# Skip weights of an S4 convolution moved from a VectorE add into the matmul group, one shared copy of the head matrices at the end, and another written-out order

## The chip, the cores and the metric

The kernel runs on one core of a Trainium2 chip. The metric is the device time of one execution in microseconds (us), the median of several runs; the kernel before takes 828.78 us (three runs, 824.48 to 829.89). The engines are TensorE (PE in the profile, its weight loads PEld), VectorE (DVE), ScalarE (ACT), GpSimd (POOL, which here issues the indirect gathers and the accumulating stores) and SyncE (SP, which issues the other DMAs).

## The reference

A layer normalisation feeds two branches, whose results are added to the input. Length 2048, width 448.

```python
def _A_ref(u, A_re, A_im, B_re, B_im, C_re, C_im, log_dt, Dskip):
    dt = jnp.exp(log_dt)[:, None]
    logdA = dt * (A_re + 1j * A_im)                       # 448 x 256 complex modes
    P = jnp.exp(logdA[:, :, None] * l[None, None, :])     # l = 0 .. 2047
    K = jnp.einsum("dn,dnl,dn->dl", Cc, P, dt * Bc).real  # one long filter per channel
    y = irfft(rfft(pad(u)) * rfft(pad(K)))[:L]            # causal convolution
    return y + u * Dskip                                  # the skip weights

def _B_ref(x, w_q, k1, k2, u, v):
    q = jnp.einsum("nd,dhc->nhc", xf, w_q)                # 16 heads, 2 halves of 256
    e = 64 * argmax(q1 @ k1.T) + argmax(q2 @ k2.T)        # one of 4096 experts per head
    act = gelu(einsum("nd,nhd->nh", xf, u[e]))
    return einsum("nh,nhd->nd", act, v[e])                # softmax over one entry is 1

xn = layernorm(x)
return x + _A_ref(xn, ...) + _B_ref(xn, ...)
```

`u * Dskip` is the same as a filter whose tap at lag 0 has Dskip added to it, and this is how both kernels do it.

## The kernel before

The work is cut into some 72 streams of steps. A step is a few instructions of one engine with the steps that it needs, the buffers that it takes and the buffers that it gives back. A string, `ORDER`, names a stream per character: in this order the steps are written, and so each engine's queue is filled. There is no scheduling at run time: an engine takes its queue in order, and an instruction whose semaphore is not there holds up everything behind it on the same engine. `Plan.run` walks the string and stops if a step stands before what it needs or finds no buffer left.

What the streams do:

- Set-up and weights (`c_*`, `par_*`, `w_*`): constants, the parameters of the modes, the query matrices multiplied with the keys.
- Branch B, scores (`ln_*`, `sc_*`, `u_*`), 16 tiles of 128 rows: normalise, transpose (L1000), score (L1019 and L1030), maximum and index on DVE and ACT. The indices go out to memory and come back.
- Branch B, experts (`e_*`, `o_*`): POOL gathers an expert's two rows per partition (L1148, 256 gathers), DVE takes the dot product (`e_d`, L1156), small steps make the gelu, PE adds the rows up (`e_p`, L1191), and POOL adds the tile to the output in memory (`o_st`, L1201).
- Branch A, filters (`s4_*`), 56 batches of 8 channels: ACT makes exponentials and sines (`s4_act`, L628, L630, L668 to L674), DVE phases and products (`s4_ph`, L653; `s4_v`, L699 to L705, into tiles `zi` and `mg`). Then the part that is changed, per batch: `s4_k1` (PE, L721) sums the products over the modes in 32 matmuls with 32 columns of weights each, into a tile of 128 x 128 in PSUM (`kp`, one of the three `kv` tiles); `s4_k2` (ACT, L729) copies 126 of the 128 columns to `kt`; `s4_k2b` (DVE, L732) adds the skip weights `dsk` to the other two columns, one for each group of four channels, writes them to `kt`, and gives back the PSUM tile; `s4_k3` (PE, L742) does the first stage of the Fourier transform on `kt`, and `s4_k4` (ACT, L746) copies it out.
- Branch A, convolution (`cv*`, `cu*`): in four chunks of channels, 128, 128, 128 and 64 wide. Products in the frequency domain (L846, L858; in the last chunk L805, L824, L832), the first inverse stage (`cv5`, L881 and L876), and its store to memory (`cv7`, tensor `t_d`).
- Branch A, end (`f_*`), per chunk four groups: SP loads a piece of `t_d` (L1214) and a piece of the head matrices `h` (L1216, 128 KB, two buffers `hl`); PE does the last stage (`f_p`, L1224); ACT copies (`f_a`, L1228); POOL adds it to the output in memory (`f_st`, L1233).

Every f32 matmul stands in the trace as two weight loads and two matmul passes.

Of the kernel before, what the change touches and what calls it, by code (L numbers as in the profile page):

```python
# [115 lines left out]
class Plan:  # L116
# [65 lines left out]
    "4444144HHHH0IIIIIIII2I2I4I2211412I264122622J4J7272HH1H7HLM2788LMLMII2L8MI444I22ZIII272I2844C4I4KOZ4IH4354C444443CPHH4DHN"  # L182
    "I46D4EEDEIJLCJCC779I79794M787DFD89L77FDFI7ECD4E79CEFEF4DK497C4N4EF44FDM84CR4CLEC9FZZD4878RQ44447DFEADCII7HHHHI97FR97I7K4"
    "M8K4IIIIIIIJD8EC5FLEC6FECDFDE7SSEDFFEFRRR77S9IIIAMOPSR9AxAAxANcQZZIIISSSTUUUIUURRIRBNJHHSSRRSIOSdIGPcxLRSSSTUUUUUUUUUHVW"
    "RWRaHRXGbISISMYRReIOIgSSIfIIIIfIKIPaxRLYGchhfSISRgSfTMRRyyyhhgIyfSSRQQzzRzOUzUyy!#!hh#yhK$gS$yJ%JPSzzyyhzz!LUSUhS#!JSThR"
    "y#Uiz$i$RyyUihh%yyyUUSRUUShURMRzZRzzS!#!OUhQ#UN$$UyyS%zSzzzSSifVWPhLWiRgRy!jTRx#f#H!$Ufh$U%SRifUSUhgMKJySRfiROKUhxhzGxyS"
    "SXxhkPzdiQzz!yYhS##SL!$$&zyMz%LTyzizUMe!j#hyUyzU!hHLy#UU$RUl$%UzRyiyUibzMKNdZUizLyRQyykhhhfSHeHMgL!#!VzzfRhiSlMLfzyS#fIN"
    "zhjRWyM!Yfg$#IRS#!IxhS$KS%I$SIihOgTIWI$PzhI%xNLRiUzIUIhcihIhRhMULQxxUI&hmmRNyyUzzyyy!yS##!$$%ziSZzzizkXRRMnihjSlhiSnHgRO"
    "y!YyahSzyyyy(J#f#Shkhgy!z$$%fflzzSPizhh!#fyjgR!hQiz#ZzLmkThlUidR$fUzMHiHHLRU$%IUyhReM!#IUSjI!#Uhh$hJh$%yISkUSUxIRbLKNhhU"
    "iy&cxlgRSMnOVhihPSy(yyyyyYizfzxcxzmzSg!S##iW!ThL1Rjnz$hIImUfz$kzz!U#fU%UyyyymNRlIUIMniySWRgSzfIRRI#zfQyROy!ShhI$i$%SzzZh"  # L190
    "zziZzhm!PJxSh##nzL!!$i#h#!$ShyMiS$Ri$Thj%HRnHxhL%MHRgNxUJfSiRLkhhgfUfiSyfUaiUlShUUSfhXiMRgKyROQxSiHzSIPRzSThUyhihjhkhUIy"
    "yIUyQyIIIRzdUzI&UzULMIeUSUzbIIjzzRlIhhkhR!SR#iSfyzhgRy!NKf#ahS$zh$ifygShN%OhgISJfSyy%VPLRhTf(zyyzRiMLUhMmhQiWiRzUylzizhn"
    "hizUmihSUyRh!#S#!hn$ym$UUjURnhyf%SifkySSlfUWJxYzfSiK%ROjghPNSyUyiymyhLnfgRhMLhgRT&xYQizRxxiziUzUzizyzz!MhUR#!yhjdyhz#$$%"
    "UzyySSR(RSzzU%hhkzyNyxiySbSkyOeSjSlPzRlihxRgzyiTXUixSzRRUShhh!khhgRylaUSUmnmR#UV!SyhfixzmOUSzUf#cS$zf$iU%S%hjyznWfiiWnUf"
    "gPKcTUzkyizhhhRRUySRhjSRRRiizhhQkhlmSlmUiyz!##yyyzyzoh!&hngh$$%yzhSSzSnzSiVfU%opgyfzTypyhzzqrhpgqphyUqhyrrifyq!rfi#f#hjs"
    "ooo!xi$i$%tkUythjyyhiyhihlbUpqkliiUyXrhhpfqg%pijhprhqfiqkghrixfrYohpdq&epgfriszfzxoxqhhhhzyUlzUzzzytjyyzhrpa!#z!#W$oW$zp"
    "zqhhtqzuyzyyUrhrgz%%pkzUfyhzflhqsif!hghihrUf#Uifitptpigi!qhyyy#pqmmi$r$i(yhyhhnyyyyhnj%kqmnhm%jnxyibhkuhrrlghszihhtxxxtV"
    "yKYylzzzyghzifziziWzzihmmfnngjiQhhkd!f#fzyyhefhiz&hyzzzlzh!hzuy!h#$i$#ifu#fica!hyjkghhl$y%ixj)g)$fxhfkh%ighhifhih**%%++h"
    "hmnixbzhhyzyyyyzYxzlizyiziz(jghhyykhz!mnyyyf&i(,dfijzifziz#lfzegkhhz#yygzlifh!hzhzh!$$mjmknhhn%hi#!mnhiil#hmn%ghhii)*+xg"
    "$hhijigyz$kff(cYfxx%%yziyyyyyyyzy(haflfhhjhhhy,yhghyhkhhyyxzzzbWiizz!iifglfmy,yfiz#!fzzi#iihhm&nzngjh$hhjf$khzh%kXao%dol"  # L200
    "zilmmhn)nzpxpoehqhyiizpgirypiqrf!f#qqph!hxxcrq#*+pry$$%fyhqpgjhrpqhYfzfgrpyrqsihhkhqhhi%tthzrihzplsXjdqhyriixczibztrtopi"
    "phifeqgzz,ihqhyyrufrzpqpqyy!krgphhflyupgm#rsfcYzfqyizhjyyy!&hqihhttrnkhzhhzrhhjsmanttklz#z$zziu$gh%iif%imffilhgf!ifinmhh"
    "ghjhdhb#i!e#y(knh$$yxhhxhxhyx%luhjg%hzhgkziyizyiyyyyyzzzyyhyhfifzmzizflyfzfigy!nz#yiimh)hhnhhjzk*+zhlhhhzmnjg)hhgz!kiz!#"
    "ififfi&f#!#$ljhhg)$iii$ifyk$%hjhhy,hhkhya*hhl*++%%hbixmnxghh%Y&xilgiijhhcfkiffgiifzhzhfihyhyjdkexzhyyyhzlhzzzmz!yy)nhhyy"
    ",yyz*ylg+hziiziifzhfzf#!yj#fiaghhfzz$y,ykzg!$i#yi#hihhm%%!hmhhnhnhbj$ik$hxdle%zYxog%iiizfljfhhgkhhgyixilmhnzf(ifihhmyfma"
    "xoyy,ynyjkzznlhmmznnzizhhpiqirpppqh!gijrhqhqprfipyhhyrqifpgqirph#!horgfsz#y&hzfzqhqh$f$%hrzyprhttpkijz%ilq(yyghqhzrhyhsb"
    "zh(rzfptktipxilhif!q#rqghrjohgfisok!hhf#fv$pihhixuohilthtqyyz$%yjgyphhhwq%iphhiripgkiffqiiuxrilqohhfzrfrfm&gnhvhijhhsmik"
    "hmhljtthhxvuizouzn(yyii)yyyyvhnkyiyizyyjwwilimnmknlmjwzmznklmzzzyyn(znpz!p#rp#rszzzz!tt!*+$rr#!p$s#)r$r$rr*ttsttstt+%u)u"
    "*%)%,*%&++,uu,(,))*+,)*)**+++,,,")


class Kernel:
# [473 lines left out]
    def products(s, b, B, e_, c1, c2, VK, col, u):  # L686
# [24 lines left out]
        def k1():  # L711
# [3 lines left out]
            for gi in range(G):  # L715
                n = 0
                for t in range(2):
                    for ri in range(2):
                        for c in range(4):
                            m = 32 * (NB * t + 4 * gi + c)  # L720
                            s.nc.tensor.matmul(kp[32 * c:32 * c + 32, 64 * gi:64 * gi + 64], T[ri][:, 1024 + m:1056 + m],  # L721
                                               view(T[ri], m, [[512, 2], [1, 32]]), start=(n == 0), stop=(n == 3))
                        n += 1


        j0 = JB[0]

# [570 lines left out]
```

## Time and profile before

| | |
|---|---|
| median of 3 runs | 828.78 us (824.48 to 829.89) |
| the profiled execution | 835.38 us, of which 833.6 us from the first to the last instruction |
| TensorE clock granted, mean | 0.892 of full speed |
| PE busy | 690.1 us, 83% of the span |
| DVE busy | 668.2 us, 80% |
| ACT busy | 546.2 us, 66% |
| POOL busy | 358.8 us, 43% |

The times of rows are from the profiled execution, which took 0.8% more than the median of the other runs. A row of a group gives the engine, the operation, the tile written and the tiles read, the shapes, the count, the busy time in us with the mean in ns of one instruction, and behind the bar how long the engine had been idle just before these instructions and what ended that. Matmuls overlap, so the busy time of a group of matmuls is less than count times mean. In a table by windows, each engine's busy time in the window stands with its count of instructions, then the granted clock, the share of DMA time and GB/s.

### The profile page before, as it was taken

The numbers are of one execution on the slowest core, as the hardware profiler recorded it, in microseconds if no ns is written. First come the engines' busy times: TensorE is split into PE (matmuls) and PEld (weight loads), VectorE is DVE, ScalarE is ACT, GpSimd is POOL, SyncE is SP. The second block draws the span as 40 slices with busy tenths as digits, with TensorE's granted clock in tenths as the row PEclk, the third lists the DMA queues.
The fourth block names the chain that finished last, engine by engine and source line by source line (L and its number), as shares of the span: only waits on it lengthen the run. The fifth ranks groups of instructions, "written<-read, shape, count | busy, mean of one in ns | idle before, by whom it ended". The sixth has DMA issues, their size and how long they took to land. (4 is left out here: it accounts for less than half of the span.)

```text
span 833.6 us, 19632 instructions
## 1 busy us (share of the span) xinstructions
PE 690.1 (83%) x7628; PEld 376.0 (45%) x7628; DVE 668.2 (80%) x1595; ACT 546.2 (66%) x1087; POOL 358.8 (43%) x307
## 2 busy tenths in 40 slices
PE   1999999999899997989989667758987777797982
PEld 0333443343444443434556344436753543675761
DVE  6695679999699998769889598878996988798630
ACT  5685337577485774544667486778895988796621
POOL 3101053547253555145425617674545286454214
PEclk9999999999899999889989876679995866998895
DMA  8998297889687769385886958999989599879679
GB/s 260 391 325 334 92 301 255 301 287 306 218 248 255 243 177 310 84 271 181 295 290 195 350 176 272 338 303 279 259 264 324 149 289 283 261 215 282 190 174 137
DMA packets 119093, 211.82 MB, mean 254 GB/s; under 512 B 38936, under 2 KB 94232, under 8 KB 118936
## 3 DMA queue, kind: packets, MB, share of 16 engines
q0 software_dynamic: 31232, 124.80, 48.1%
q1 hardware_dynamic: 87768, 85.77, 32.7%
q8 instruction: 60, 0.98, 0.5%
q14 instruction: 33, 0.27, 0.1%
HBM read 180.90 MB, written 33.29 MB: 257 GB/s over the span
## 5 line engine op out<-in xcount | busy, mean ns | idle before, releaser
L1148 POOL DMA_INDIRECT q<-in_uv_dram,ig x256 | 308.7, 1206 | 378.3 <-PE po L1191 154.5
L1019 PE MATMUL s<-q,xt 128*128 128x512 f32 x384 | 183.8, 619 | 1.8 <-ACT xt L1003 1.6
L1156 DVE SCALAR_TENSOR_TENSOR q<-q,xr 128x448 f32<-128x448 f32 x256 | 153.0, 621 | 5.1 <-DMA q<-in_uv_dram,ig 4.9
L1019 PEld LDWEIGHTS s<-q,xt 128*128 128x128 f32 x384 | 71.0, 194 | 94.5 <-issue 90.3
L721 PE MATMUL kv<-mg 128*32 128x64 f32 x1792 | 79.9, 245 | 32.2 <-issue 17.0
L721 PE MATMUL kv<-zi 128*32 128x64 f32 x1792 | 84.2, 244 | 18.1 <-issue 17.8
L628 ACT ACTIVATE mg<-kv 128x512 f32<-128x512 f32 x112 | 62.9, 601 | 30.1 <-PE kv L617 16.5
L721 PEld LDWEIGHTS kv<-mg 128*32 128x32 f32 x1792 | 52.4, 123 | 63.4 <-issue 34.7
L1191 PE MATMUL po<-q,A 128*32 128x448 f32 x512 | 69.5, 619 | 6.3 <-DVE A L1179 3.1
L721 PEld LDWEIGHTS kv<-zi 128*32 128x32 f32 x1792 | 56.9, 126 | 25.7 <-issue 25.6
L701 DVE TENSOR_TENSOR zi<-mg,CS 128x1024 f32<-128x1024 f32 x56 | 68.4, 1221 | 0.0
L705 DVE TENSOR_TENSOR mg<-mg,CS 128x1024 f32<-128x1024 f32 x56 | 68.3, 1219 | 0.0
L653 DVE CUSTOM_DVE_ANT_0 ph<-st,ph 128x512 uint16<-128x512 uint16 (+2 forms) x84 | 65.1, 775 | 0.2
L674 ACT ACTIVATE CS<-CS,halfpi 128x1024 f32<-128x1024 f32 x56 | 64.5, 1152 | 0.9
L1045 DVE TENSOR_REDUCE mx<-s 128x8 f32<-128x512 f32 x64 | 43.9, 686 | 25.3 <-PE s L1030 18.8
L668 ACT ACTIVATE CS<-ph 128x1024 f32<-128x1024 int32 x56 | 62.6, 1118 | 1.9 <-DVE ph L653 1.6
L671 ACT ACTIVATE CS<-ph 128x1024 f32<-128x1024 int32 x56 | 62.8, 1121 | 0.0
L742 PE MATMUL kv<-f,kt 128*64 128x128 f32 x448 | 41.2, 317 | 16.4 <-ACT mg L628 5.0
L765 PE MATMUL tp<-q,f 128*128 128x448 f32 x64 | 36.1, 648 | 19.5 <-DMA f<-in_f_dram 16.1
L699 DVE SCALAR_TENSOR_TENSOR zi<-mg,CS 128x512 f32<-128x512 f32 x56 | 38.6, 689 | 14.7 <-ACT CS L668 8.6
L617 PE MATMUL kv<-lc,rt 32*128 32x512 f32 x112 | 36.8, 568 | 14.1 <-ACT mg L628 7.1
L881 PE MATMUL s<-q,e 64*128 64x256 f32 x192 | 48.2, 404 | 0.0
(205 smaller groups left out, 1314.6 us busy)
## 6 DMA issues: line engine op xcount, KB each, us to landing
q<-in_wq_dram SPq DMA_DIRECT2D x32, 448.0 KB
xr<-xn_d SPq DMA_DIRECT2D x64, 224.0 KB
vu_d<-q SPq DMA_DIRECT2D x64, 112.0 KB
q<-vu_d SPq DMA_DIRECT2D x12, 512.0 KB
t_d<-q SPq DMA_DIRECT2D x24, 256.0 KB
q<-t_d SPq DMA_DIRECT2D x12, 512.0 KB
q<-in_uv_dram,ig POOLq DMA_INDIRECT x256
q<-in_x_dram SPq DMA_DIRECT2D x16, 224.0 KB
```

What stands on the lines that cost most here:

```text
L628: s.nc.scalar.activation(mg[:, :2, i], ps.rearrange("p (k n) -> p k n", k=2), AF.Exp)
L653: s.nc.vector.tensor_tensor(out=rw(n, 2 * n), in0=rw(0, n), in1=o["st"][:, k, b0:b0 + 2].rearrange("p b h m x -> p (b h m x)")[:, None].to ...
L668: s.nc.scalar.activation(CS[:, 1].rearrange("p (m r x) -> p m r x", r=16, x=2), four(s.ph), AF.Sin, scale=SC)
L671: s.nc.scalar.activation(B["CS"][:, 0].rearrange("p (m r x) -> p m r x", r=16, x=2), four(s.ph), AF.Abs)
L674: s.nc.scalar.activation(B["CS"][:, 0], B["CS"][:, 0], AF.Sin, scale=-SC, bias=s.halfpi)
L701: V.tensor_tensor(out=zi[:, 512:], in0=mg[:, 512:], in1=CS[:, 1], op=ALU.mult)
L705: V.tensor_tensor(out=mg[:, 512:], in0=mg[:, 512:], in1=CS[:, 0], op=ALU.mult)
L721: s.nc.tensor.matmul(kp[32 * c:32 * c + 32, 64 * gi:64 * gi + 64], T[ri][:, 1024 + m:1056 + m], view(T[ri], m, [[512, 2], [1, 32]]), start ...
L1019: s.nc.tensor.matmul(B["sc", q].rearrange("p a b -> p (a b)"), B["xt"][:, i], w, start=(q % 2 == 0 and i == 0), stop=(q % 2 == 1 and i == 2))
L1148: s.nc.gpsimd.indirect_dma_start(out=ue, out_offset=None, in_=s.io["uv"], in_offset=bass.IndirectOffsetOnAxis(ap=s.IDX[t][:, c, g:g + 1].b ...
L1156: s.nc.vector.scalar_tensor_tensor(Q["ue", g, c][:, :D], Q["ue", g, c][:, :D], 1.0, B["xr", c], op0=ALU.mult, op1=ALU.mult, accum_out=Q["d ...
L1191: s.nc.tensor.matmul(B["po"][32 * c:32 * c + 32, :D], Q["A"][:, g - g0, c], Q["ue", g, c][:, D:], start=(g == 0), stop=(g == 3))
```

## The change

Three edits.

First, `s4_k2b` is gone. Behind each group's 16 matmuls, `s4_k1` issues one more matmul that accumulates into the same PSUM tile: the 128 x 128 identity as weights, one column of `dsk` as the moving operand, one output column. So there are 112 such matmuls, and 56 DVE instructions fewer. `s4_k2` copies all 128 columns and gives back the PSUM tile; `s4_k3` waits for `s4_k2`.

Second, for the last two of the four chunks the head matrices come in one load of 512 KB (`f_h`), into one of the large `q` buffers, and the eight loads of 128 KB are gone; the buffer is held until the last `f_p`. The first two chunks load as before.

Third, the string `ORDER` is another one: 3217 steps where there were 3272 (56 `s4_k2b` fewer, one `f_h` more). Only its first line is shown.

```diff
 ORDER = (
-    "4444144HHHH0IIIIIIII2I2I4I2211412I264122622J4J7272HH1H7HLM2788LMLMII2L8MI444I22ZIII272I2844C4I4KOZ4IH4354C444443CPHH4DHN"
...
+    "4HH4HHIIIIIIIII1I1Z2I22220414IJJ14412142222274LM44LMLHMLHHH665M422222227424443K4C7788478H8II4OIIPDI44I3KI44NII44I47Z444I"
...
                             s.nc.tensor.matmul(kp[32 * c:32 * c + 32, 64 * gi:64 * gi + 64], T[ri][:, 1024 + m:1056 + m],
-                                               view(T[ri], m, [[512, 2], [1, 32]]), start=(n == 0), stop=(n == 3))
+                                               view(T[ri], m, [[512, 2], [1, 32]]), start=(n == 0), stop=False)
                         n += 1
-        j0 = JB[0]
+                s.nc.tensor.matmul(kp[:, 64 * gi + JB[0]:64 * gi + JB[0] + 1], s.ident, s.dsk[:, G * b + gi:G * b + gi + 1], start=False, stop=True)
 
         def k2():
-            s.nc.scalar.activation(B["kt"].rearrange("p (g j) -> p g j", g=G)[:, :, :j0], B["kp"].rearrange("p (g j) -> p g j", g=G)[:, :, :j0], AF.Copy)
-
-        def k2b():
-            s.nc.vector.tensor_tensor(out=B["kt"].rearrange("p (g j) -> p g j", g=G)[:, :, j0], in0=B["kp"].rearrange("p (g j) -> p g j", g=G)[:, :, j0],
-                                      in1=s.dsk[:, G * b:G * b + G], op=ALU.add)
+            s.nc.scalar.activation(B["kt"], B["kp"], AF.Copy)
             s.rel(B["kp"])
...
-        a1 = p.add("s4_k2", "ACT", ac(126), k2, deps=[a])
-        a = p.add("s4_k2b", "DVE", dv(2) + 4, k2b, port=False, deps=[a1, s.dskip_done], give=("kv",))
+        a = p.add("s4_k1", "PE", 1170, k1, deps=[v, s.dskip_done, s.C["ident"]], take=("kv", "kt"), give=("zi", "mg"))
+        a = p.add("s4_k2", "ACT", ac(128), k2, deps=[a], give=("kv",))
...
+        late = ck >= len(s.chunks) - 2
+        if ck == len(s.chunks) - 2:
+            def lh():
+                s.H = s.flat("q", "hall", 1024).rearrange("p (x e) -> p x e", e=32)
+                s.nc.sync.dma_start(s.H, s.io["h"])
+            s.h_done = p.add("f_h", "SP", xf(128, 4096), lh, deps=[s.t_done[ck - 1]], take=("ue",))
...
-                B["h"] = s.flat("hl", "hl", 256).rearrange("p (x e) -> p x e", e=32)
-                s.nc.sync.dma_start(B["h"], s.io["h"][:, 8 * g:8 * g + 8])
+                if not late:
+                    B["h"] = s.flat("hl", "hl", 256).rearrange("p (x e) -> p x e", e=32)
+                    s.nc.sync.dma_start(B["h"], s.io["h"][:, 8 * g:8 * g + 8])
```

What stands in the queues, at the places that the prediction speaks of. First PE at the `s4_k1` of the 37th batch, before (`kv` is the PSUM tile, `mg` and `zi` the products; x4 is one matmul for each of four column groups; `lc` and `rt` belong to the exponents, `ttl` to their load):

```order
L619 MATMUL kv2_106<-lc_134,rt_5026 128x256
L721 MATMUL kv0_104<-mg_5407 32x64 x4
L721 MATMUL kv0_104<-zi_5647 32x64 x4
L721 MATMUL kv0_104<-mg_5407 32x64 x4
L721 MATMUL kv0_104<-zi_5647 32x64 x4
L721 MATMUL kv0_104<-mg_5407 32x64 x4
L721 MATMUL kv0_104<-zi_5647 32x64 x4
L721 MATMUL kv0_104<-mg_5407 32x64 x4
L721 MATMUL kv0_104<-zi_5647 32x64 x4
L561 MATMUL kv2_106<-ident_123,ttl_5370 128x128 x2
```

And now, the same batch on the same engine:

```order
L616 MATMUL kv2_106<-lc_134,rt_5276 128x512
L720 MATMUL kv1_105<-mg_5416 32x64 x4
L720 MATMUL kv1_105<-zi_5677 32x64 x4
L720 MATMUL kv1_105<-mg_5416 32x64 x4
L720 MATMUL kv1_105<-zi_5677 32x64 x4
L723 MATMUL kv1_105<-dsk_131,ident_123 128x1
L720 MATMUL kv1_105<-mg_5416 32x64 x4
L720 MATMUL kv1_105<-zi_5677 32x64 x4
L720 MATMUL kv1_105<-mg_5416 32x64 x4
L720 MATMUL kv1_105<-zi_5677 32x64 x4
L723 MATMUL kv1_105<-dsk_131,ident_123 128x1
L618 MATMUL kv0_104<-lc_134,rt_5276 128x256
```

Two matmuls over the whole array have come into the batch, one behind each group of 16, and the step stands at another place among the exponents' matmuls.

Second, DVE about the same batch, before (L732 is `s4_k2b`, L1156 a dot product of the experts, L699 and L701 products of a later batch, L1166 to L1179 the small steps of the gelu):

```order
L1166 SCALAR_TENSOR_TENSOR x_5510<-x_5510,dot 128x8
L705 TENSOR_TENSOR mg<-mg,CS 128x1024
L1175 TENSOR_TENSOR dw<-dot,ig 128x8
L1172 SCALAR_TENSOR_TENSOR th<-th,dw 128x8
L1179 TENSOR_TENSOR A<-mask,th 128x256
L732 TENSOR_TENSOR kt<-kv_104,dsk 128x2
L1156 SCALAR_TENSOR_TENSOR q_80,dot<-q_80,xr 128x448
L1156 SCALAR_TENSOR_TENSOR q_79,dot<-q_79,xr 128x448
L699 SCALAR_TENSOR_TENSOR zi<-mg,CS 128x512
L701 TENSOR_TENSOR zi<-mg,CS 128x1024
```

And now (the lines are 1 to 7 lower):

```order
L1168 TENSOR_TENSOR dw<-dot,ig 128x8
L652 ISA ph<-st,ph 128x1024
L1165 SCALAR_TENSOR_TENSOR th<-th,dw 128x8
L652 ISA ph<-st,ph 128x2048
L1172 TENSOR_TENSOR A<-mask,th 128x256
L584 TENSOR_TENSOR st<-tpl,amt 128x16x32 x2
L698 SCALAR_TENSOR_TENSOR zi<-mg,CS 128x512
L1149 SCALAR_TENSOR_TENSOR q_86,dot<-q_86,xr 128x448
L700 TENSOR_TENSOR zi<-mg,CS 128x1024
```

The add is gone, and the first instruction behind the mask step that needs a result of ACT is now the product L698 (L699 before), with a step of the phases ahead of it instead of two dot products.

Third, the end of the program. POOL's last stores before (`ob` is a tile of the experts, `q` a group of the convolution; 4x128 is chunk three, 4x64 the last chunk):

```order
L1201 DMA out_dram<-ob 128x448
L1233 DMA out_dram<-q_98 128x4x128
L1233 DMA out_dram<-q_84 128x4x128
L1233 DMA out_dram<-q_103 128x4x128
L1201 DMA out_dram<-ob 128x448
L1233 DMA out_dram<-q_100 128x4x128
L1233 DMA out_dram<-q_92 128x4x64
```

And now:

```order
L1194 DMA out_dram<-ob 128x448
L1238 DMA out_dram<-q_103 128x4x128
L1238 DMA out_dram<-q_94 128x4x128
L1194 DMA out_dram<-ob 128x448
L1238 DMA out_dram<-q_90 128x4x128
L1238 DMA out_dram<-q_80 128x4x128
L1238 DMA out_dram<-q_84 128x4x64
```

The last tile of the experts (the second `ob`) is stored behind two groups of chunk three where it was behind three. On PE, too, its last matmuls stand ahead of the last `f_p` of chunk three, where one of their groups stood behind it. SP's last loads before (`t_d_116` is chunk three, `t_d_117` the last):

```order
L895 DMA t_d_117<-q_99 64x512 x2
L1214 DMA q_92<-t_d_117 128x8x64
L1216 DMA hl<-in_h_dram 128x256
L1214 DMA q_87<-t_d_117 128x8x64
L1216 DMA hl<-in_h_dram 128x256
L1214 DMA q_86<-t_d_117 128x8x64
L1216 DMA hl<-in_h_dram 128x256
L1214 DMA q_93<-t_d_117 128x8x64
```

And now:

```order
L1214 DMA q_103<-t_d_116 128x8x128
L1206 DMA q_96<-in_h_dram 128x1024
L1214 DMA q_94<-t_d_116 128x8x128
L1214 DMA q_90<-t_d_116 128x8x128
L888 DMA t_d_117<-q_83 64x512 x2
L888 DMA t_d_117<-q_97 64x512 x2
L1214 DMA q_80<-t_d_116 128x8x128
L888 DMA t_d_117<-q_79 64x512 x2
L888 DMA t_d_117<-q_99 64x512 x2
L1214 DMA q_84<-t_d_117 128x8x64
L1214 DMA q_102<-t_d_117 128x8x64
L1214 DMA q_100<-t_d_117 128x8x64
```

The one load of `h` stands behind the first load of chunk three, and the last chunk's four loads follow one another.

66 lines of the change are left out of this document (35 added, 31 removed).

## The prediction

> **What bounds the kernel now.** I read the page first, then busy time by stages, the waits, the groups of instructions, and last the timeline at single places. The chain of waits says nothing of the body: it reaches back only to 814 us. The stages say more (PE, PEld, DVE, ACT, POOL with counts, then clock, DMA share, GB/s):
>
> ```profile
> PE 690.1 (83%) x7628; PEld 376.0 (45%) x7628; DVE 668.2 (80%) x1595; ACT 546.2 (66%) x1087; POOL 358.8 (43%) x307
> 40.00:320.00 280.00, 268.67 (x1650) 113.41 (x1653) 244.51 (x618) 180.28 (x430) 105.68 (x88) 0.99 0.79 260
> 320.00:800.00 480.00, 383.62 (x5615) 244.36 (x5617) 398.57 (x926) 337.73 (x600) 233.49 (x193) 0.84 0.81 251
> 800.00:833.60 33.60, 15.82 (x296) 10.18 (x292) 0.86 (x2) 5.63 (x14) 10.18 (x9) 0.71 0.95 164
> ```
>
> From 40 to 320 us PE is busy for 268.67 of 280 us at a clock of 0.99: the score matmuls bound it. From 320 to 800 us nothing is full: DVE 83%, PE 80% at a clock of 0.84, ACT 70%. There the engines wait for one another in turn. The last 34 us are a tail of loads, small matmuls and stores.
>
> **What the add costs.** Its group, its spread over the two stages, and the waits that name it:
>
> ```profile
> L732 DVE TENSOR_TENSOR kt<-kv,dsk 128x2 f32<-128x2 f32 x56 | 8.9, 159 | 33.7 <-ACT kt L729 32.2 <-ACT mg L628 1.0 <-issue 0.4
> 40.00:320.00 280.00, 1.57 (x10) 0.99 0.79 260
> 320.00:800.00 480.00, 7.33 (x46) 0.84 0.81 251
> DVE kt L732 <- ACT kt L729: 30.0, 12, 7.3
> PE kv L742: 1.9, 1
> ```
>
> 56 adds of 159 ns are 8.9 us, 7.3 of them behind 320 us, where DVE also stood idle for 30.0 us in front of them, in 12 places (fourth row, waits of that stage). The last row is from the list of who waited for the add: PE lost only 1.9 us to it. All of 30 us is not to be had. The three longest of these waits (idle time in brackets), with ACT at the longest:
>
> ```profile
> 548.67 0.16 DVE L732 TENSOR_TENSOR kt<-kv,dsk 128x2 f32<-128x2 f32 x1 [3.39 <-ACT kt L729]
> 551.55 0.68 DVE L585 TENSOR_TENSOR st<-tpl,amt 128x512 int32<-128x512 int32 x1
> 633.39 0.16 DVE L732 TENSOR_TENSOR kt<-kv,dsk 128x2 f32<-128x2 f32 x1 [7.00 <-ACT kt L729]
> 634.69 0.69 DVE L699 SCALAR_TENSOR_TENSOR zi<-mg,CS 128x512 f32<-128x512 f32 x1
> 717.39 0.16 DVE L732 TENSOR_TENSOR kt<-kv,dsk 128x2 f32<-128x2 f32 x1 [3.68 <-ACT kt L729]
> 718.68 0.69 DVE L699 SCALAR_TENSOR_TENSOR zi<-mg,CS 128x512 f32<-128x512 f32 x1
> 632.81 0.38 ACT L565 ACTIVATE rt<-kv 128x256 fp32r<-128x256 f32 x1 [7.08 <-PE po L1191]
> 633.50 1.15 ACT L668 ACTIVATE CS<-ph 128x1024 f32<-128x1024 int32 x1
> ```
>
> At 633 us DVE waited for ACT, but ACT itself had stood for 7.08 us behind a late PE, and the sine L668 comes only then. Behind the add DVE had 634.69 - 633.55 = 1.1 us of dot products; then comes the product L699, which needs that sine. Without the add DVE does these 1.1 us early and waits at L699 instead. At 717 us the same: 718.68 - 717.55 = 1.1 us can move. At 548 us phases and dot products fill the time to 551.55 at least, 2.7 us of the 3.39. So 4.9 of 14.07 us, 35%, can be filled; the rest is ACT's and PE's lateness and reappears at L699. In the new order the product stands one phase step of this kind behind the mask step, which is no better.
>
> **The sum, part by part**, against the profiled execution of 835.4 us (span 833.6 and 1.8 around it); it is 0.8% above the median of 828.8, and the sum's difference is taken off the median.
>
> *DVE.* Relief behind 320 us: 7.3 us of adds and 35% of 30.0, 10.5, together 17.8 us. Bounds: 7.3 and 37.3. How much reaches the end is a choice: all of it if DVE were the bound, little where PE or ACT is. With DVE at 83% and PE at 80% side by side I pass 0.55: -9.8 us. In the first stage PE binds and covers the 1.6 us: nothing; were PE not the bound there, they would be gained too.
>
> *PE and ACT behind the add.* With it goes the hand-over ACT, DVE, PE: the 1.9 us for which PE waited, -1.9 (bounds 0 and twice that).
>
> *The identity matmuls.* 112 matmuls are 224 passes of 128 x 128 weights and one column. No row shows one column; the nearest, with the batch's own matmuls by stage last:
>
> ```profile
> L1000 PE MATMUL tp<-ident,q 128*128 128x128 f32 x64 | 10.2, 283 | 0.0
> L1000 PEld LDWEIGHTS tp<-ident,q 128*128 128x128 f32 x64 | 8.0, 147 | 10.0 <-issue 8.6 <-ACT pw L485 1.4
> L1019 PE MATMUL s<-q,xt 128*128 128x512 f32 x384 | 183.8, 619 | 1.8 <-ACT xt L1003 1.6
> 40.00:320.00 280.00, 14.86 (x704) 11.89 (x704) 0.99 0.79 260
> 320.00:800.00 480.00, 86.61 (x2880) 63.84 (x2880) 0.84 0.81 251
> ```
>
> A pass with 128 columns holds PE for 10.2 / 64 = 159 ns, one with 512 columns for 183.8 / 384 = 479 ns; so 0.83 ns a column, and 159 - 127 x 0.83 = 54 ns at one column, an estimate. 224 x 54 ns = 12.1 us of PE. The low end is a pass of the packed 32-column matmuls, (14.86 + 86.61) / 3584 = 28 ns, 6.3 us; the high end a pass that neither its load nor its drain hides, 147 + 283 = 430 ns, 96 us. A gain is excluded: the passes come on top, in the same queue. I take 54, since identity, weights and shape are those of L1000, which lies between the packed and the bare pass. By the packed matmuls' counts 11 of 56 batches lie in the first stage (704 of 3584): 2.4 us there count in full. The other 9.7 lie in a stage where PE is idle for a fifth of the time; a quarter of it passes, 2.4. Together +4.8 us. The idle time of PE is the cover; without it 12.1.
>
> [...]
>
> *The tail.* First the chain, then ACT, POOL, PE and SP:
>
> ```profile
> 814.35 1.42 DMA out_dram<-ob
> 815.77 5.63 issue
> 821.40 0.04 POOLq L1233
> 811.98 0.54 ACT L1198 ACTIVATE ob<-po 128x448 f32<-128x448 f32 x1 [4.73 <-PE po L1191]
> 813.59 1.27 POOL L1233 DMA_DIRECT2D out_dram<-q  x1 [4.77 <-ACT q L1228]
> 822.05 3.92 POOL L1233 DMA_DIRECT2D out_dram<-q  x3 [6.29 <-issue]
> 809.87 1.08 PE L1224 MATMUL kv<-q,hl 64*32 64x128 f32 x32
> 813.73 0.53 SPq L1214 DMA_DIRECT2D q<-t_d  x1
> 816.26 0.34 SPq L1216 DMA_DIRECT2D hl<-in_h_dram  x1
> 818.70 0.34 SPq L1216 DMA_DIRECT2D hl<-in_h_dram  x1
> ```
>
> The last tile of the experts was put out at 814.35, and the next store, to the same rows of the output, went at 822.05, 7.7 us later, with four behind it. In the new order one `f_p` (1.08 us) no longer stands ahead of that tile on PE, and one store of 813.59 no longer stands ahead of it on POOL (about 1.2 us between tile ready, 812.52, and its turn): -2.3 us if the 7.7 stay as they are. Shared `h` takes away SP's stops at 816.26 and 818.70 (2.5 and 2 us, for a buffer `hl`), so that the last four groups are ready ahead of POOL: that alone moves nothing, since POOL is later, but it keeps the gain. Its 512 KB go through SP ahead of the loads of chunk three, whose groups wait for it; at the 164 GB/s of that stage they take 3 us beside PE's work. I take -2.5. Bounds: 0, if the store's own 7.7 us stretch, and -5.
>
> *The order.* Its other effect is taken at nothing. What hides it: the steps are those of before. What it may do is bounded by the waits of DVE outside the add in the long stage, 480 - 398.6 - 30 = 51 us: a fifth of them, 10 us, either way.
>
> Sum: -9.8 - 1.9 + 4.8 - 2.5 = -9.4 us. 828.8 - 9.4 = 819.4, rounded to 819.
>
> **Rivals.** Changes below 1%, 8.3 us, can hardly be told from none.
>
> *The waits only move (28%).* For it: at 633 us ACT had been waiting as long as DVE. Then only the 7.3 us of adds remain, at 0.55 a gain of 4.0 instead of 9.8, and the hand-over gains nothing: 828.8 - 4.0 + 4.8 - 2.5 = 827. Against it: at 548 us there is work to fill the wait.
>
> *The waits go altogether (14%).* All 37.3 us of relief at 0.55, 20.5, instead of 9.8: 808 to 809. For it: the order may have put ready work ahead of every late one. [...] Against: ACT's own waits stay.
>
> *The identity loads break up the packed matmuls (17%, slower).* A load of all 128 columns may wait for the four column groups ahead of it and hold up the four behind it. With c ns a pass, a fifth in full and the rest at a half (the wait then lies in the batch's own chain), it costs 224 x c x 0.6; it eats the 14.2 us of gains from c = 106 ns on and makes the kernel slower by over 1% from 167 ns. Half of the bare 430 ns, 215, costs 28.9 us: 828.8 + 14.7 = 843 to 844. For it: PEld's 147 ns a load at L1000. Against: the same loads with their matmuls took 159 ns a pass, columns and all. [...]
>
> *The add isn't gone* can be left out: the queues show it gone.
>
> **The numbers.** The forecast has 41%; its own range, with the order's 10 us and the smaller bounds, is 808 to 831. The range over all is 807 to 838: it takes in the first rival, half of the second, and leaves out the most of the slower one. Faster by over 1%, below 820.5: somewhat over half of the forecast's 41% and nearly all of the second rival's 14, and some of the first's by the order, 0.42. Slower by over 1%, above 837: most of 17 and a little of the first, 0.18. Within: 0.40.
>
> **What would show it.** Right: DVE busy near 659 us; DVE's idle time behind 320 us down by 8 to 15 us and found at L698 and at the products of the convolution; the identity's passes near 54 ns of PE each; the last tile of the experts 2 us nearer to the last convolution matmul. Wrong: passes of over 100 ns, or a batch's sums that take much more than the 1.35 us (14.86 / 11) of the first stage; DVE's idle time unchanged; or waits for gathers on DVE, which the trace of before hardly has, by the new order.

## The result, and the profile after

The changed kernel is slower: 852.81 us (median of 4 runs, 851.28 to 860.5) against 829.34 us of the kernel before in the same session. The ratio is 1.0322, with a 95% interval of 1.0231 to 1.0413; like all ratios below it compares the runs in the faster of two states alone, so it is not the quotient of the two medians. The profiled execution took 854.22 us, 852.2 of them from the first to the last instruction. The forecast was 819.

First the page's busy times and the long stages of the kernel after, then the places where DVE waited in the long stage, behind 320 us:

```profile
PE 734.4 (86%) x7852; PEld 415.2 (49%) x7852; DVE 662.5 (78%) x1539; ACT 549.9 (65%) x1089; POOL 359.3 (42%) x307
```

```profile
40.00:320.00 280.00, 267.67 (x1574) 115.33 (x1574) 228.32 (x575) 170.18 (x401) 100.32 (x87) 0.98 0.76 248
320.00:800.00 480.00, 410.52 (x5485) 265.69 (x5484) 392.44 (x872) 344.00 (x609) 235.31 (x191) 0.83 0.81 249
```

```profile
DVE zi L698 <- ACT CS L667: 18.5, 5, 7.7
DVE q L851 <- ACT us L846: 18.3, 10, 5.9
```

And three rows of the same stage before:

```profile
DVE q L858 <- ACT us L853: 10.5, 9, 1.8
DVE zi L699 <- ACT CS L668: 8.6, 4, 4.8
DVE x L1166 <- ACT x L1163: 2.6, 4, 0.9
```

DVE does 5.7 us less than before (668.2), less than the 8.9 us of the add, since other groups took a little longer. But PE does 44.3 us more (690.1). In the long stage PE went from 383.62 to 410.52 us busy, while fewer of its instructions lie in that stage (5485 for 5615): the work has moved to the right, out of the stage. DVE's 30.0 us of waits at the add are gone, and two other waits have grown: at the product behind the sine from 8.6 to 18.5 us, and at the product of the convolution (`L851`, before `L858`) from 10.5 to 18.3.

Next the new group itself, matmul and weight load, and the page's chain of waits by line, which in this execution reaches back to the start and so says more than that of before:

```profile
L723 PE MATMUL kv<-dsk,ident 128*128 128x1 f32 x224 | 48.9, 286 | 0.5 <-issue 0.5
L723 PEld LDWEIGHTS kv<-dsk,ident 128*128 128x128 f32 x224 | 39.2, 219 | 13.8 <-issue 6.2
```

```profile
PE s L1012 21%; PE kv L720 10%; PE po L1184 6%; PE s L1023 4%; PE s L839 4%; PE kv L723 4%; PE kv L736 4%; PE tp L758 4%; PE s L874 4%; PE kv L616 3%; PE kv L909 2%; ACT CS L667 2%; ACT CS L670 2%; PE kv L618 2%; ACT CS L673 1%
```

One column of output holds PE for 48.9 / 224 = 218 ns a pass, four times the 54 ns of the forecast, and the identity matmuls are 4% of the chain, some 34 us. PE lines hold most of the chain.

The timeline shows where the time of one such matmul lies. This is PE at 301 us of the kernel after, at full clock (granted 1.00 from 300 to 302.5 us); x8 are eight passes in a row, and they overlap, so one reads the distance of the starts:

```profile
300.71 0.32 PE L720 MATMUL kv<-mg 128*32 128x64 f32 x8
300.85 0.29 PE L720 MATMUL kv<-zi 128*32 128x64 f32 x8
300.96 0.29 PE L720 MATMUL kv<-mg 128*32 128x64 f32 x8
301.07 0.29 PE L720 MATMUL kv<-zi 128*32 128x64 f32 x8
301.30 0.38 PE L723 MATMUL kv<-dsk,ident 128*128 128x1 f32 x2
301.61 0.32 PE L720 MATMUL kv<-mg 128*32 128x64 f32 x8
```

Eight packed passes follow one another every 0.11 us, so the identity's two passes would begin at 301.18; they begin at 301.30, 0.12 us late, and the packed ones go on at 301.61. Between 301.18 and 301.61 lie 0.43 us, in which PE would have done some thirty packed passes. It is not this place alone: over the whole trace the first load of an identity matmul begins a median of 148 ns behind the start of the packed pass ahead of it. What fills this gap no view shows; of two other shapes below one has it and one does not.

### The profile page after: what moved, and what is told of

It is laid out like the page before. It is cut to its first block, busy times and chain, and to the rows that moved or that the text cites. A ratio compares the mean times of both kernels' runs of the same rounds, so it can differ in the third digit from the quotient of the medians.

```text
span 852.2 us, 19988 instructions
## 1 busy us (share of the span) xinstructions
PE 734.4 (86%) x7852; PEld 415.2 (49%) x7852; DVE 662.5 (78%) x1539; ACT 549.9 (65%) x1089; POOL 359.3 (42%) x307
## 4 chain that ended last, share of the span: by engine, by line
PE 72%; ACT 13%; issue 6%; DVE 4%; DMA 2%; another core or an unknown queue 1%; POOL 1%; SPq 0%; POOLq 0%; ACTq 0%; DVEq 0%
PE s L1012 21%; PE kv L720 10%; PE po L1184 6%; PE s L1023 4%; PE s L839 4%; PE kv L723 4%; PE kv L736 4%; PE tp L758 4%; PE s L874 4%; PE kv L616 3%; PE kv L909 2%; ACT CS L667 2%; ACT CS L670 2%; PE kv L618 2%; ACT CS L673 1%
## 5 line engine op out<-in xcount | busy, mean ns | idle before, releaser
L1012 PE MATMUL s<-q,xt 128*128 128x512 f32 x384 | 186.8, 626 | 2.6 <-ACT xt L996 1.7
L720 PE MATMUL kv<-zi 128*32 128x64 f32 x1792 | 79.4, 244 | 12.4 <-issue 12.3
L720 PEld LDWEIGHTS kv<-mg 128*32 128x32 f32 x1792 | 48.7, 121 | 41.6 <-issue 29.0
L698 DVE SCALAR_TENSOR_TENSOR zi<-mg,CS 128x512 f32<-128x512 f32 x56 | 38.6, 690 | 30.7 <-ACT CS L667 18.5
L720 PEld LDWEIGHTS kv<-zi 128*32 128x32 f32 x1792 | 53.9, 126 | 17.5 <-issue 17.3
L736 PE MATMUL kv<-f,kt 128*64 128x128 f32 x448 | 43.7, 330 | 19.9 <-ACT mg L627 13.0
L851 DVE TENSOR_TENSOR q<-us,s 128x512 f32<-128x512 f32 x48 | 32.3, 683 | 25.3 <-ACT us L846 18.3
```

What stands on the lines that cost most here:

```text
L736: s.nc.tensor.matmul(vp[64 * ri:64 * ri + 64, 128 * gi:128 * gi + 128], B["kt"][:, 64 * gi:64 * gi + 64], s.f1[:, ri], start=True, stop=True)
L1012: s.nc.tensor.matmul(B["sc", q].rearrange("p a b -> p (a b)"), B["xt"][:, i], w, start=(q % 2 == 0 and i == 0), stop=(q % 2 == 1 and i == 2))
```

## The experiments

The runs fell on several chips of two kinds: on one kind the kernel before takes 824 to 830 us, as in the forecast's runs ("the first kind"), on the other 762 to 764 ("the second kind"). Each ratio is against the kernel before on the same chip.

**Theories.** A: the identity passes cost what they hold of PE, and about half of that reaches the end (the third rival of the forecast). B: the new order is at fault, and the passes happen to be there. C: the shared copy of the head matrices.

**The identity matmuls alone, and both orders without any skip weights.** The first kernel is the kernel before with the first edit only, in the old order (the `s4_k2b` steps struck from the string). The other two leave the skip weights out, in the new order and in the old. In all three, and in every later version without the add, `s4_k2` copies all 128 columns and gives back the PSUM tile, as in the kernel after.

```diff
 # old order, identity matmuls: edit one alone
+s.nc.tensor.matmul(kp[:, 64 * gi + JB[0]:64 * gi + JB[0] + 1], s.ident, s.dsk[:, G * b + gi:G * b + gi + 1], start=False, stop=True)
-p.add("s4_k2b", "DVE", ...)
 # new order without skip weights: the kernel after, and
-s.nc.tensor.matmul(kp[:, 64 * gi + JB[0]:64 * gi + JB[0] + 1], s.ident, ...)
 # old order without skip weights: the kernel before, and
-p.add("s4_k2b", "DVE", ...)
```

> The order of before with the identity matmuls in place of the DVE add (56 steps taken out of the string, the head loads as before). Theory A (the identity passes cost it: 224 passes of 218 ns in the trace of the changed kernel, 48.9 us of PE): 842 to 856 us, and L-row of the identity again near 49 us. Theory B (the new order costs it, the identity is hidden): 818 to 830 us.

> The changed kernel without the 112 identity matmuls: the skip weights are left out of the computation. Theory A: PE loses 49 us of busy time and the time falls to 810 to 828 us. Theory B: it stays at 838 to 852 us, since the order is what costs.

> The kernel before without the DVE adds: the skip weights are left out of the computation, the order of the other steps is unchanged. It measures the add by itself. If DVE's waits in front of the add go altogether: 800 to 812 us. If they only move, as the prediction's first rival has it: 821 to 829 us. By the prediction's own step (17.8 us of relief, 0.55 of it passed on, and 1.9): about 817.

Measured: old order with identity matmuls 1.025 (1.0159 to 1.0341); new order with none 0.9981 (0.9944 to 1.0019); old order with none 0.9894 (0.9842 to 0.9946). Later the two in the old order were run again, both on one other chip of the first kind, and the new order with none on a third:

> The old order with the identity matmuls, nothing else changed. On the 763 us chip: if the cost goes by the line's TensorE time, as in the new order (46 us of it, 3 per cent), 1.015 to 1.025 over before; if the new order is what makes the passes dear there, 1.00 to 1.01. On the 824 us chip it repeats 1.016 to 1.034.

> The kernel before with the skip weights left out (no add, no identity matmul; the output is short of them by intent). If this falls on a chip where the kernel before takes about 763 us: it is the base that the pieces in the old order lacked. If the passes cost by their TensorE time in the old order as in the new, the ratio is 0.985 to 0.992 (pieces at 28 us of TensorE stood at 1.0024, at 14.7 us at 1.0052). If the pieces cost nothing in the old order, it is about 1.00. On a chip where before takes 824 us it repeats 0.984 to 0.995.

> The new order without identity and without add once more (the skip weights are left out), with more rounds, to size the order against the old order without add, which was 0.9894 of before. If the new order and the shared head are worth nothing: 0.989 to 0.993. If the new order is itself worse by 1%: 0.996 to 1.002.

Measured: identity in the old order 1.0379 (1.0339 to 1.042), none in the old order 0.9976 (0.9942 to 1.0011), none in the new order 0.9995 (0.9923 to 1.0068). The same edit moves by about 1% from chip to chip, more than its intervals, so differences are best taken within one chip. The result's own chip is known only by its kind. The passes in the old order cost 1.025 - 0.9894 = 3.6% on the one and 1.0379 - 0.9976 = 4.0% on the other, 29 and 33 us, each within one chip; in the new order 1.0322 less 0.9981 or 0.9995 is 3.3 to 3.4%, 27 to 28 us, a difference across chips that has a like within one chip of the second kind below (3.05%). That is theory A, and B falls: the passes cost as much in the old order. The group in the old order, from the first of these runs, has the size of the one after:

```profile
L724 PE MATMUL kv<-dsk,ident 128*128 128x1 f32 x224 | 50.2, 292 | 2.5 <-issue 2.5
```

Where the add alone is gone (old order with none), the waits of DVE in the long stage read:

```profile
DVE x L1159 <- ACT x L1156: 12.2, 6, 5.2
DVE q L851 <- ACT us L846: 9.8, 6, 6.0
DVE zi L699 <- ACT CS L668: 9.5, 4, 4.9
```

The 30.0 us at the add are gone, and 12.2 us (14.2 in the second run) stand at another small step of the experts that before waited 2.6 us: so some of the wait was time that ACT lacked and only moved, as the first rival had it. The gain of 0.2 to 1.1%, 2 to 9 us, is what removing the add brought; the interval of the first run reaches 1.6%, that of the second 0.6%.

**The head matrices alone.** The kernel before with the second edit only, `f_h` written right behind the first load of chunk three.

```diff
+s.h_done = p.add("f_h", "SP", xf(128, 4096), lh, deps=[s.t_done[ck - 1]], take=("ue",))
 ...
+if not late:                                   # late: chunks three and four
     s.nc.sync.dma_start(B["h"], s.io["h"][:, 8 * g:8 * g + 8])
```

> The kernel before with the shared head matrices alone (the DVE add and the order of before kept, the one load of 512 KB put in behind the first load of chunk three). By the prediction's step on the tail, where SP's stops alone move nothing because POOL is later: within 1.5 us of before. If the eight loads and their two buffers set the end: 3 to 7 us faster.

Measured: 1.0011 (0.9969 to 1.0052), from 3 us faster to 4 us slower. C falls.

**Fewer or smaller passes in the old order.** In the first, one identity matmul per batch with two output columns in place of two with one; in the second, four tiles of 32 x 32 on the diagonal, which is all of the identity that is not zero. In every version with these matmuls once per batch, the second group of 16 also no longer opens with a clearing flag of its own (`start=(gi == 0 and n == 0)`).

```diff
 # one per batch, behind both groups
+s.nc.tensor.matmul(view(kp, JB[0], [[64, G]]), s.ident, s.dsk[:, G * b:G * b + G], start=False, stop=True)
 # four diagonal tiles per batch
+for c in range(4):
+    r = slice(32 * c, 32 * c + 32)
+    s.nc.tensor.matmul(view(kp[r], JB[0], [[64, G]]), s.ident[r, r], s.dsk[r, G * b:G * b + G], start=False, stop=True)
```

> The order of before, no DVE add, and one identity matmul per batch instead of two: it stands behind all 32 matmuls and has two output columns, one per group (for this the second group no longer opens with its own clearing flag). Theory A, in which each full-array matmul costs by breaking the packed stream (0.41 us at full clock in the trace of the changed kernel, two passes of 205 ns): half of the 49 us of PE, and a time half way between 821 without any and 850 with two, 833 to 839 us. Rival C, in which any matmul behind the group costs by the length of the batch's own chain, not by count: 844 to 852.

> As the run with one identity matmul per batch of two columns, but cut into four tiles of 32 x 32 on the diagonal of the array, one per group of 32 rows. Theory A: the tiles pack behind the 16 matmuls and break nothing; the line is busy for under 15 us and the time comes to 822 to 831 us. Rival C, or a cost by the number of PE instructions as the run with four packed pieces of each identity suggests: 836 to 850.

Measured: one per batch 1.0069 (1.002 to 1.0118), with 25.1 us of PE in the line; diagonal tiles 0.9978 (0.9931 to 1.0025), 16.6 us:

```profile
L724 PE MATMUL kv<-dsk,ident 128*128 128x2 f32 x112 | 25.1, 291 | 0.4 <-issue 0.4
```

```profile
L726 PE MATMUL kv<-dsk,ident 32*32 32x2 f32 x448 | 16.6, 183 | 5.2 <-issue 5.0
```

Half the passes take half of the PE time (25.1 for 50.2) and land between none and all, as measured on other chips: 1.0069 between 0.9894 to 0.9976 and 1.025 to 1.0379, a little faster than the 833 to 839 us that were expected. A second column costs nothing that shows (25.1 / 112 = 224 ns a pass, and 50.2 / 224 = 224 with one column); the passes do. The diagonal tiles put the kernel level with the one before, with somewhat more PE time than the 15 us that were expected. Their timeline, in the same format as above, has the same gap ahead of them:

```profile
187.91 0.29 PE L721 MATMUL kv<-mg 128*32 128x64 f32 x8
188.02 0.29 PE L721 MATMUL kv<-zi 128*32 128x64 f32 x8
188.25 0.24 PE L726 MATMUL kv<-dsk,ident 32*32 32x2 f32 x8
```

188.25 is 0.12 us behind the 188.13 at which another packed group would have begun. So the gap isn't the load of 128 columns: a 32-column tile of another shape has it too, and over its trace the median from packed pass to first load is again 148 ns.

**The identity in the packed shape.** Four pieces of the identity, 128 rows by 32 columns, the shape of the packed matmuls, behind each group; first in the new order.

```diff
+for c in range(4):
+    s.nc.tensor.matmul(kp[32 * c:32 * c + 32, 64 * gi + JB[0]:64 * gi + JB[0] + 1], s.ident[:, 32 * c:32 * c + 32], s.dsk[:, G * b + gi:G * b + gi + 1], start=False, stop=True)
```

> The changed kernel with each identity matmul cut into four, one for each group of 32 output rows, with 32 columns of the identity as weights, so that they have the shape of the 16 matmuls ahead of them. Theory A in the form that the load of the whole array holds up the packed matmuls: 448 records of 32 columns each cost near 28 ns, about 12 us of PE and more by count, and the time falls to 818 to 832 us. If a one-column pass costs by its own drain and not by its load, PE keeps its 40 to 50 us in this line and the time stays at 845 to 856. Theory B: 845 to 856 too, but with the line's busy time down.

Measured: 1.0297 (1.0233 to 1.0361), hardly less than the full passes. Its timeline at full clock:

```profile
294.91 0.29 PE L720 MATMUL kv<-zi 128*32 128x64 f32 x8
295.02 0.22 PE L724 MATMUL kv<-dsk,ident 128*32 128x1 f32 x8
295.08 0.30 PE L720 MATMUL kv<-mg 128*32 128x64 f32 x8
```

Here there is no gap: the pieces begin 0.11 us behind the group ahead of them and are over in 0.06 us, where the full identity took 0.43. Over the trace the first load of the pieces begins a median of 2 ns behind the packed pass ahead. That is what the expectation was built on, and it holds. But it didn't make the kernel faster, and the line's busy time is not small, 34.7 us (it counts the whole of a pass, the overlapped part too):

```profile
L724 PE MATMUL kv<-dsk,ident 128*32 128x1 f32 x896 | 34.7, 178 | 8.6 <-issue 8.4
```

The expectation reckoned with 448 pieces; as f32 matmuls they are 896 passes, and in front of them, unlike the full ones (0.5 us), PE also stood for 8.4 us with nothing that the profile shows to wait for ("issue"). By the letter of the expectation, 848 us with a line that is less busy is what theory B foretold; but the new order with none, 0.9981 on the same chip, has ruled B out. The stalls by "issue" in the batch sums as a whole were these in the new order with none:

```profile
PE kv L720 <- issue: 31.8, 76, 1.3
```

With the pieces they are 34.0 + 8.4 = 42.4 us, with the full passes 24.5 + 0.5 = 25.0. So the pieces add 34.7 us in their line and 10.6 of stalls, 45 us, and the full passes add 48.9 and take away 6.8, 42 us. By this sum the two are alike, as their times are. It is rough, since the stalls of one kernel differ by 10 us from run to run (26.8 and 37.4 with the full passes in the old order), and no run shows that it is the cause. So the gap is a part of the price of the full identity, and not all of what these kernels lose.

**The second kind of chip.** The next runs, with pieces and then with the changed kernel again, fell on the second kind. There the stalls by "issue" are few: 0.7 to 8.5 us in the batch sums of all its traces, against 25 to 42 on the first kind. The rows of PE's waits, from the kernel before on the first kind, and then from the pieces in the old order on the second:

```profile
PE kv L721 <- issue: 34.8, 87, 1.1
```

```profile
PE kv L721 <- issue: 0.7, 1, 0.7
```

With "once per batch" the four pieces stand behind both groups, with two columns, as in the run with one full matmul per batch.

> The order of before, no DVE add, and once per batch, behind all 32 matmuls, four pieces of the identity of 128 rows and 32 columns with two output columns: the same shape of weights as the matmuls ahead, so the array keeps its division into four column groups. Theory D (every change of the array's division drains it, about 148 ns ahead and 95 to 180 ns behind, as the records of the 32 x 32 tiles and of the full identity show; the load itself is small): PE's line is busy for under 10 us, the ratio comes to 0.988 to 0.997 of before, better than the 32 x 32 tiles' 0.998. Rival E (PE instructions by themselves cost, as four packed pieces twice per batch did with 1.030 in the new order): 0.998 to 1.012.

> The changed kernel (its order and its shared head) with the same packed pieces once per batch, behind all 32 matmuls, two columns. Theory D: 0.994 to 1.006 of before, near the new order without any (0.998). Rival E: 1.008 to 1.02, half of what the pieces cost twice per batch (1.030).

> The order of before with the packed pieces of one column behind each of the two groups of 16, as the run in the new order that came to 1.030. If that cost belongs to the pieces (16 more weight loads and passes in the middle of the batch): 1.015 to 1.025 here. If it was the new order's: 0.992 to 1.003.

Measured: pieces once per batch 1.0052 in the old order (1.002 to 1.0085) and 0.9944 in the new (0.9909 to 0.9979); pieces behind each group in the old order 1.0024 (0.9988 to 1.006). In their order these three lie in the ranges of E, of D, and of a cost that belongs to the new order (D and E as the texts above name them; the traces show the gap of 148 ns, not that it is a drain): they do not agree on one theory, and the expectations were worked out from ratios of the first kind. Then, to see all forms in the new order side by side:

> The changed kernel again, beside the three others of its order. If the drain at the identity passes is the cause by itself, it loses on every chip: 2 to 4% over before, and PE's line of the identity is busy for 42 to 50 us. If the loss comes by PE's supply of instructions, it is under 1% on a chip where that supply is good (before at 762 us), and 3% where it is not (before at 824 us).

> The new order with four packed pieces of one column behind each group, 896 passes. By the drain alone (the pieces keep the array's division): under 1% over the new order without any, on every chip. By the supply of instructions: 3% over it where the supply is poor, under 1% where it is good.

> The new order with the four packed pieces once per batch, two columns, 448 passes. By the drain alone: within 0.6% of the new order without any. By the supply of instructions: half way between none and 896 passes.

> The new order without identity and without add (the skip weights are left out): the base line of this group. 0.993 to 1.002 of before on a chip of the first kind, as measured twice; on the other kind 0.985 to 0.995, since the packed pieces once per batch came to 0.994 there.

Measured, from none to full, with the line's busy time and PE's total:

| new order, second kind of chip | ratio | the line | PE in all |
|---|---|---|---|
| none | 0.9878 (0.9802 to 0.9953) | 0 | 641.5 us |
| pieces once per batch | 0.9949 (0.9901 to 0.9997) | 14.2 us | 643.1 |
| pieces behind each group | 1.0107 (1.0045 to 1.017) | 28.5 | 657.9 |
| full identity, the kernel after | 1.0183 (1.0117 to 1.0248) | 46.0 | 681.1 |

The full passes cost 1.0183 - 0.9878 = 3.05% or 23 us here: with the stalls all but gone (2.9 us, and 1.5 with none), they cost nearly what they cost on the first kind. So their price is not the stalls. The pieces behind each group still cost 2.3%, though no gap stands ahead of them; so it is not the gap alone either. These pieces have some stalls, 5.6 us ahead of the packed matmuls and 2.9 ahead of the pieces, 8.5 us in all and less than the 17.5 us that they cost:

```profile
L724 PE MATMUL kv<-dsk,ident 128*32 128x1 f32 x896 | 28.5, 177 | 2.9 <-issue 2.9
```

Neither of the two single causes that I set against each other for these runs, the drain and PE's supply of instructions, of which the traces show only the stalls by "issue", fits. What fits is that PE's time in the line goes to the end by about a half: 5.4 us of 14.2, 17.5 of 28.5, 23 of 46.0. It is no more than a fit: the intervals leave the first of these three open by some 7 us either way, and by PE's total, the last column, the rises are 1.6, 16.4 and 39.6 us, of which no such share passes on.

A row at a lower granted clock adds one number. In the changed kernel on this chip, PE at 452 us (granted clock 0.50 from 452 to 454.5 us):

```profile
452.68 0.44 PE L720 MATMUL kv<-mg 128*32 128x64 f32 x8
452.89 0.44 PE L720 MATMUL kv<-zi 128*32 128x64 f32 x8
453.27 0.59 PE L723 MATMUL kv<-dsk,ident 128*128 128x1 f32 x2
453.78 0.44 PE L720 MATMUL kv<-mg 128*32 128x64 f32 x8
```

The packed groups come every 0.21 us, about half as often as at full clock (0.11), and the identity matmul takes from 453.10 to 453.78, 0.68 us. Of its 224 passes 176 lie between 320 and 800 us, where such stretches are (mean granted clock 0.88, against 1.00 from 40 to 320).

**The cheapest form on the first kind of chip.** Pieces once per batch in the new order beat the kernel before on the second kind, 0.9944 and 0.9949. On the first:

> New order, shared head, skip weights as four pieces of 128 rows by 32 columns once per batch, two columns each. On the 763 us chip it repeats 0.990 to 0.998. On the 824 us chip: leaving the skip weights out gave 0.998 to 1.000 there, and pieces behind each group, 34.7 us of TensorE, gave 1.030; at half the passes the ratio by TensorE time is 1.012 to 1.017, so slower than before. If the gain of the other chip carries over, 0.99 to 1.00.

Measured: 1.0162 (1.0116 to 1.0208), the other sign. Its rows:

```profile
L720 PE MATMUL kv<-zi 128*32 128x64 f32 x1792 | 81.4, 243 | 20.7 <-issue 20.0
L720 PE MATMUL kv<-mg 128*32 128x64 f32 x1792 | 76.9, 243 | 21.5 <-issue 16.4 <-DVE mg L704 3.3 <-ACT kt L729 0.7
L724 PE MATMUL kv<-dsk,ident 128*32 128x2 f32 x448 | 18.3, 181 | 4.1 <-issue 4.1
```

20.0 + 16.4 + 4.1 = 40.5 us of PE's time in the batch sums went into stalls, where the same kernel on the second kind of chip has 7.7 (and on the first kind the new order with none has 31.8). So for small passes the two kinds differ, and here the stalls are the likely cause; a run that takes them away on one chip was not tried. Of the versions that compute the skip weights only this one and the changed kernel ran on both kinds, and neither beats the kernel before on both. The diagonal tiles in the old order are level with it on the first.

## Why the prediction was wrong

| term | forecast | measured |
|---|---|---|
| add removed, with the hand-over | -11.7 us | -2 to -9 us (old order without skip weights, two chips) |
| identity matmuls | +4.8 | +27 to +33 (both orders, first kind of chip; +23 on the second) |
| tail, with the head matrices | -2.5 | -3.4 in the trace; the head alone 0 (-3 to +4) |
| order | 0, either way 10 | 0 to +8 (+7 within one chip), with head and tail in it |
| sum | -9.4 | +26.7 (1.0322 of 829) |

**The identity matmuls: the step that failed.** The forecast took 54 ns a pass, the value at one column of a straight line through L1000 and L1019, "which lies between the packed and the bare pass". Measured: 218 ns. Of the two rows of that straight line, L1000 is not the matmul that the forecast took it for ("identity, weights and shape are those of L1000"). Its passes are transposes: five per tile of 128 rows and one pass each, 64 + 16 in the trace, and so an exception to the two passes of an f32 matmul. What is loaded there is a slice of `q`, and the identity is the moving operand: the fifth slice is 64 wide, and the 16 loads with 64 columns are its. Only the size of the load was the same. And both rows stand in runs of passes with whole-array neighbours, L1000 in fives, L1019 mostly in sixes and twelves; at 81.80 us of the trace before, the one follows the other without a gap. In such a run the loads lie beside the passes: those of L1019, of 128 x 128, are busy for 71.0 us beside 183.8 us of its own passes, in front of which PE stood for 1.8 us. A single 128 x 128 matmul between 128 x 32 ones had a gap of 0.12 us ahead of it, and its two loads began 0.11 us apart. The bare pass, half of which the third rival took, 215 ns, was the better row, and the rival's price, 28.9 us, lies within what was measured. In part that is luck: the half was a choice, and of the rival's mechanism only the break in the packed stream was seen, not that the width of the load makes it (a 32-column tile has the same gap). The rival's chance of 17% was too low; "the same loads with their matmuls took 159 ns a pass" spoke against it only for a run of such passes.

The other figure of that term, a fifth in full and a quarter of the rest, was too small as well: 27 to 33 of 48.9 to 50.2 us reach the end, 0.55 to 0.67, where the forecast's shares come to 0.4 (4.8 of 12.1). The rival's 0.6 holds. The idle fifth of PE in the long stage was taken as cover; but of its 96.4 us before, some 55 are PE waiting for ACT and DVE and 38.7 are stalls by "issue"; and a batch's sums that end later can make all behind them later. DVE's wait at the convolution's product shows it: in the long stage it is 9.8 and 7.1 us in the old order with none and 17.4 and 17.0 with the passes, and in the new order 13.9 and 15.5 with none and 18.3 with them. The wait at the product behind the sine does not show it: 9.5 and 17.9 us in the old order with none, 10.8 and 20.1 with the passes. An estimate from the distance of the loads puts them at half of the line: at full clock the second load of an identity matmul begins 108 or 109 ns behind the first, and 224 times that is 24 us of the 48.9. The busy time, 39.2 / 224 = 175 ns a load at a mean clock of 0.88, is longer than that distance. To the loads come the gap ahead, 148 ns, and the way back into the packed stream, 180 ns from the second pass to the next packed one (medians of the trace after).

**The add.** The mechanism was right: with the add gone, DVE's busy time is where it was said to be (662.5 for 659), and part of the waits reappears elsewhere. The size was off: -11.7 for -2 to -9 (the interval of the first chip still holds -11.7, that of the second does not). Most of the waits moved, as the first rival said.

**What DVE's waits were to show.** I expected its idle time behind 320 us to fall by 8 to 15 us. It rose, from 480 - 398.6 = 81.4 to 480 - 392.4 = 87.6 us. With none of the skip weights it is 71.9 and 78.0 us in the new order, and 86.7 and 87.2 in the old one: there removing the add did not lower it at all. With the passes in the old order it is 97.1 and 98.8. So in both orders the passes add some 10 to 16 us to it. (The stretch from 320 to 800 us holds somewhat other work in each kernel, so these differences are rough.)

**The tail.** The last copies of the convolution on ACT and the last stores on POOL, after:

```profile
828.43 0.38 ACT L882 ACTIVATE q<-tp 128x256 f32<-128x256 f32 x1
833.64 0.88 POOL L1194 DMA_DIRECT2D out_dram<-ob  x1 [1.40 <-ACT ob L1191]
840.85 3.90 POOL L1238 DMA_DIRECT2D out_dram<-q  x3 [5.01 <-ACT q L1233]
```

and the copy before:

```profile
806.37 0.38 ACT L889 ACTIVATE q<-tp 128x256 f32<-128x256 f32 x1
```

From the last copy to the end were 833.6 - 806.75 = 26.9 us and are 852.2 - 828.81 = 23.4: 3.4 us gained for 2.5. The last tile of the experts is put out 4.8 us behind that copy, before 7.6, as foreseen, and its store still holds the next one off for 7.2 us (before 7.7).

**The order.** Nothing was taken for it, 10 us either way. With none of the skip weights the new order, with the shared head, is 0.9% slower than the old within one chip of the first kind (0.9981 against 0.9894), and 0.1 to 1.0% slower by all four runs (0.9995 and 0.9976 are of two other chips); with the full passes the two are the same within what was measured (1.0322 against 1.025 and 1.0379). On the second kind it is 1.1% faster with pieces once per batch (0.9944 against 1.0052, one chip) and 0.8% slower with pieces behind each group (1.0107 against 1.0024, two chips). The bound held for the measured differences, and its sign is not settled.

**What stays open.** How much of the passes' price is the gap ahead of them: the pieces behind each group cost 2.3% with no gap and 8.5 us of stalls. Whether they cost that in the old order too, since the second kind of chip has no run of the old order with none. And what makes the stalls and the 8% between the two kinds of chip.

## What to carry to other kernels

A matmul of one column was not small among packed neighbours here: 218 ns of PE a pass, where the batch's packed passes took 28 in the kernel before. If its tile shape differs from theirs, price it by the break that it makes in the stream, read from a place where shapes change, and not by a straight line through runs of one shape; and the neighbours' own shape does not make it free (2 to 3% here, behind each group). Before work is moved from one engine to another, run the kernel with that work left out: here it showed 0.2 to 1.1% to be had, less than what the new place cost. An engine that is idle for a fifth of a stage was no cover here for work that others wait for: about half of what was put on it, or more (0.55 to 0.67 on the first kind of chip), reached the end.

## What was not expected of the hardware

- The gap of 0.12 us in the packed stream of 128 x 32 tiles was the same ahead of a 128 x 128 and of a 32 x 32 tile, and absent ahead of another 128 x 32 one (the three timelines above; over the traces 148, 148 and 2 ns from packed pass to next load, in the median). One full f32 identity matmul took 0.43 us out of the packed stream at full clock, 0.68 at a granted clock of 0.50, and four pieces of the packed shape 0.06.
- Two kinds of chips ran the same kernel before in 824 to 830 us and in 762 to 764. On the first, PE stood for 34.8 us in the packed matmuls with nothing that the profile shows to wait for, on the second for 0.7 (with the pieces added; 0.7 to 8.5 by version). One and the same kernel, pieces once per batch in the new order, was 0.5% faster than before on the one and 1.6% slower on the other: a gain of half a per cent is one of a chip until it is seen on another.
